# Seven products instead of eight for the second product of a token pair, with the third block's work moved between the pair's groups

## The chip, the cores and the metric

The kernel runs on one core of one Trainium2 chip. The metric is the device time of one execution in microseconds (us). All times here are of that one core. The engines are named as the profile names them: PE (TensorE, matrix products), PEld (its weight loads), DVE (VectorE), ACT (ScalarE), POOL (GpSimd) and SP (SyncE, which issues the transfers). L341 is line 341 of the kernel.

## The reference

Attention with a local window and block summaries feeds a first network of two gates, and that feeds a second network. The change concerns only the second network:

```python
def _moe2_ref(x, w_in, w_out):          # x: 1536 x 512, w_in: 512 x 2048, w_out: 2048 x 512
    h = x @ w_in
    relu6 = np.clip(h + 3.0, 0.0, 6.0)
    g = h * relu6 / 6.0
    return (g @ w_out).astype(np.float32)
```

The first network is `a = x @ w1; b = x @ w2; h = a * b @ w3; h @ w_out`, where `w3 @ w_out` is multiplied out beforehand in the kernel. The weights come as 64-bit numbers and are turned into 32-bit ones on the chip.

## The kernel before, in words

**Numbers.** Each 32-bit operand of a product is kept as a high and a low part (a slot of the arena holds both, 128 x 2 x 512), and `products` (L334 to L348) does three matmuls of 128x128 by 128x512 for each product of tiles: high by high, low by high, high by low. A high part is an ACT copy (L295, L555), the low part a subtraction on DVE or POOL (L298, L560). Twelve matmuls are the unit `GRP`.

**Stages.** The 1536 tokens are three blocks of 512. (1) Weights of the first network are multiplied out and the attention of the first block runs. (2) `ab` and `acc1` work through the first network, block after block, eight steps of 36 matmuls each, while the attention of the next block runs between; `x2_out` (L589) writes the block's result back as high and low parts. Meanwhile `convert_out` (L318) turns the 16 tiles of the second network's `w_out` into high and low parts and stores them in DRAM (`wo`). (3) The second network's first product for blocks 0 and 1 goes by Strassen's scheme, in eight groups q (L858 to L906): seven half products of 6 matmuls each in place of eight, on weight sums that `w_in_group` (L788) makes from two `w_in` tiles, and on token sums that `sums_of_x` (L772) makes once. `copied` (L825), `added` (L829) and `gated` (L835) put the seven results together, apply the gate and split it in high and low parts. Two of the four gated tiles of a group (block 0) go straight into `acc2` (L622), the second product, in the next group; the two of block 1 are stored in DRAM (`gj`), and so are the plain `w_in` tiles (`wi`). So a group is 42 matmuls of the first product and 24 of block 0's second product. (4) Block 2: 16 steps `hu` (L603, 12 matmuls) and 16 `acc2` (12 matmuls). (5) Block 1: 16 `acc2` on gated tiles read back from `gj`. The result of block 0 is written by `y_out` (L627) after the second `hu`, that of block 2 after its last `acc2`, that of block 1 at the end.

**Order of the work.** All instructions go into a list with an engine, an estimated duration and a due time; `Graph.schedule` (L92 to L150) simulates the engines and writes out one fixed order for each engine's queue. Only matmul groups bring their own due time; that of every other instruction follows from the matmuls that need it:

```python
        due = [o[2] if o[0] == "pe" else self.LAST for o in self.ops]
                due[i] = min(due[i], due[u] - self.ops[i][1] - self.LAT.get(e, 40))
```

Instructions marked `lock` (all of POOL, and DVE with its operands in SBUF) are simulated one at a time. On the chip each engine takes its queue in this order, and an instruction that waits holds all behind it.

Of the kernel before, what the change touches and what calls it, by code (L numbers as in the profile page):

```python
# [56 lines left out]
N_LATE, N_TMP = 4, 8  # L57
N_RAW, N_C = 4, 4


class Graph:
# [6 lines left out]
    LAT = {"sp": 2100, "pe": 250}  # L68
# [86 lines left out]
DUE_K, DUE_V, DUE_ROWS = 106.6, -119.0, -31.9  # L155
# [5 lines left out]
AHEAD, BEHIND = -27.8, -143.7  # L161
HOLD = 6000.0
OUT_AT, OUT_STEP = 180, 6.5


def build(tc, qd, kw, vw, kt, vt, consts, wp_in, w12_in, w2_in, out):
# [417 lines left out]
    def acc1(due, i, gs):  # L584
        for c in range(4):
            terms = [(wslice(A_WP + i, c * P), lambda h: slot(gs)[:, h, :])]
            products(due + c, terms, bank[c], c, both(A_WP + i) + both(gs), i == 0, i == NFC - 1)
# [14 lines left out]

    def hu(due, j, swin, gs):  # L603
        xs = A_X + NPAIR * j
        n = chain["n"]
        chain["n"] += 1
        b = 4 + n % 2
        terms = [(wslice(swin, k * P), lambda c, k=k: ar[:, xs + k, c, :]) for k in range(4)]
        products(due, terms, bank[b], b, both(swin) + [k for p in range(4) for k in both(xs + p)])
        t, u = ta[n % 2], tg[n % 2]  # L610
        g.op("act", 600, due, lambda: nc.scalar.activation(out=t, in_=bank[b], func=AF.Relu, bias=three),  # L611
             [("bank", b), "three"], [("ta", n % 2)])
        g.op(
            "dve", 685, due,
            lambda: nc.vector.scalar_tensor_tensor(  # L615
                out=u, in0=t, scalar=6.0, in1=bank[b], op0=ALU.min, op1=ALU.mult
            ), [("bank", b), ("ta", n % 2)], [("tg", n % 2)],
        )
        split(due, u, ("tg", n % 2), gs)
        return gs  # L620
# [60 lines left out]
    with tc.manual_schedule():  # L681
# [47 lines left out]
        for j in range(NBLK):  # L729
            for i in range(NFC):  # L730
                gs = ab(due, j, i)
                due += 2 * GRP
                if pend:
                    acc1(due, pend[1], pend[2])
                    if pend[1] == NFC - 1:
                        x2_out(due, pend[0])
                    due += GRP
                pend = (j, i, gs)
# [14 lines left out]
        def tile_of(n):  # L753
            return n // 2 + NFC * (n % 2)

        wo_slot = [A_LATE + i for i in range(N_LATE)] + [A_WP + i for i in range(NFC)]
        n_wo = len(wo_slot)
# [4 lines left out]
        half = GRP / 2  # L762

# [5 lines left out]
        def f32s(s, h):  # L769
            return lambda: slot(s)[:, h, :].bitcast(F32)  # L770

        def sums_of_x(due):  # L772

            for k in range(2):
# [7 lines left out]
                for n, o, a, b in ((1, 1, 0, 1), (3, 0, 2, 0), (2, 2, 2, 1), (4, 3, 3, 2)):  # L782
                    tensors(due, tf[o], tf[a], tf[b], ALU.subtract, fs[a], fs[b], fs[o])
                    s = tslot[n][k]
                    to_hi_lo(due, 1, tf[o], [fs[o]], lambda s=s: slot(s)[:, 0, :], lambda s=s: slot(s)[:, 1, :],
                             [("t", s, 0)], [("t", s, 1)], "dve")

        def w_in_group(due, q):  # L788

            w = [A_W2 + 4 * (q % 2) + i for i in range(4)]  # L790
            src = []
            for i in range(2):
                r, c, parts = to_f32(due, w2_in[q + NFC * i])
                src.append((lambda c=c: cs[c].bitcast(F32), ("c", c)))
            for i in range(2):
                src.append((lambda i=i: tmps[6 + i], ("f", 6 + i)))
            (a, ka), (b, kb), (e, ke), (f, kf) = src
            lo, hi = slice(0, TB // 2), slice(TB // 2, TB)
            for out, ko, x, kx, op, y, ky in (
                ((e, lo), ke, (b, lo), kb, ALU.add, (b, hi), kb),  # L800
                ((e, hi), ke, (e, lo), ke, ALU.subtract, (a, lo), ka),
# [108 lines left out]
        for n in range(n_wo - 8):  # L910
            at[n] = A_X + n
# [114 lines left out]
```

## Time and profile before

| | |
|---|---|
| Median of three runs | 572.25 us (569.72 to 572.67) |
| The profiled execution | 572.83 us, of which 570.9 us are the span from its first to its last instruction |
| PE busy | 537.8 us |
| DVE, ACT, POOL busy | 344.8, 281.9, 216.1 us |

Read the table of the engines first (who is busy), then the busy time by stage (where PE has gaps), then the chain of work that ended last (what the end hangs on), and only then the durations of single instructions. The columns of the views are named where they stand, in the section of rows.

### The profile page before, as it was taken

What the parts mean: (1) busy time and instruction counts of PE and PEld (TensorE: products, weight loads), DVE (VectorE), ACT (ScalarE), POOL (GpSimd) and SP (SyncE); (2) the same over time, 40 slices, a digit from 0 to 9 for tenths busy, and PEclk for the clock granted to TensorE, in tenths of its full rate; (3) what the DMA queues carried; (4) which work ended last, traced back from release to release, by engine and by line L of the source; (5) the groups of instructions that cost most, each with busy time, mean ns of one, the idle gap of its engine ahead of it and who ended that gap; (6) DMA issues with size and microseconds to landing.
All of it is one profiled execution on the core that took longest, in us unless ns stands there. A gap on an engine that the chain in (4) does not pass through costs nothing.

```text
span 570.9 us, 8140 instructions
## 1 busy us (share of the span) xinstructions
PE 537.8 (94%) x3032; PEld 437.3 (77%) x3032; DVE 344.8 (60%) x464; ACT 281.9 (49%) x483; POOL 216.1 (38%) x178
## 2 busy tenths in 40 slices
PE   0579999999989999999998999999999999999997
PEld 0457778887868887888886788888888888888885
DVE  5899977947673477879785888887645222220000
ACT  2688877535342445555646877775545222222001
POOL 0578646695431135377044866555100000000000
PEclk9999999999999999999999999999999999999999
DMA  8999883664232364568777857843499831002622
GB/s 308 379 356 324 240 269 105 189 204 153 70 92 86 111 214 145 182 228 258 249 258 261 291 205 288 299 169 148 148 337 419 312 110 38 1 0 85 203 82 73
DMA packets 42111, 112.62 MB, mean 197 GB/s; under 512 B 4040, under 2 KB 13512, under 8 KB 42072
## 3 DMA queue, kind: packets, MB, share of 16 engines
q1 hardware_dynamic: 41928, 111.97, 57.7%
q8 instruction: 24, 0.39, 0.3%
q10 hardware_dynamic: 144, 0.13, 0.1%
q14 instruction: 15, 0.12, 0.1%
HBM read 82.17 MB, written 28.31 MB: 194 GB/s over the span
## 4 chain that ended last, share of the span: by engine, by line
PE 83%; DMA 6%; DVE 4%; POOL 3%; ACT 2%; issue 2%; SPq 1%; ACTq 0%; DVEq 0%; POOLq 0%
PE bank L341 77%; PE bank L525 2%; DMA raw<-in_w_dram 2%; PE bank L463 2%; PE bank L510 1%; DMA kres<-in_kt_dram 1%; DMA qst<-in_q_dram 1%; POOL arena L298 1%; DMA wo<-raw 1%; DVE c L286 1%; POOL sc L500 1%; ACT c L267 0%; SPq L239 0%; DVE bank L282 0%; DVE sc L474 0%
## 5 line engine op out<-in xcount | busy, mean ns | idle before, releaser
L341 PE MATMUL bank<-arena 128*128 128x512 f32 x1152 | 278.2, 394 | 2.5 <-POOL arena L298 1.1
L341 PEld LDWEIGHTS bank<-arena 128*128 128x128 f32 x1152 | 214.6, 189 | 50.4 <-POOL arena L298 2.3
L341 PE MATMUL bank<-arena,w 128*128 128x512 f32 x816 | 196.6, 391 | 2.7 <-ACT ta L577 2.0
L341 PEld LDWEIGHTS bank<-arena,w 128*128 128x128 f32 x816 | 152.3, 188 | 36.2 <-ACT ta L577 2.9
L560 DVE TENSOR_TENSOR arena<-tg,arena 128x512 fp32r<-128x512 f32 x68 | 56.1, 825 | 26.3 <-ACT arena L555 25.5
L555 ACT ACTIVATE arena<-tg 128x512 fp32r<-128x512 f32 x72 | 45.1, 628 | 40.8 <-DVE tg L579 23.5
L282 DVE SCALAR_TENSOR_TENSOR c<-c,raw 128x512 uint32<-128x512 uint32 x48 | 45.0, 944 | 16.7 <-ACT raw L273 16.4
L298 POOL TENSOR_TENSOR arena<-c,arena 128x512 fp32r<-128x512 f32 (+1 forms) x34 | 42.0, 1249 | 33.5 <-ACT arena L295 33.5
L267 ACT ACTIVATE c<-raw 128x512 f32<-128x512 f32 x48 | 31.7, 665 | 33.2 <-DMA raw<-in_w_dram 27.2
L286 DVE SCALAR_TENSOR_TENSOR c<-raw,c 128x512 uint32<-128x512 uint32 x48 | 47.8, 1011 | 0.2
L273 ACT ACTIVATE raw<-raw 128x512 uint32<-128x512 uint32 (+1 forms) x72 | 46.8, 660 | 0.0
L341 PE MATMUL bank<-late,arena 128*128 128x512 f32 x192 | 46.6, 389 | 0.0
L298 POOL TENSOR_TENSOR raw<-c,raw 128x512 fp32r<-128x512 f32 x16 | 22.0, 1380 | 56.4 <-ACT raw L295 55.0
L341 PEld LDWEIGHTS bank<-late,arena 128*128 128x128 f32 x192 | 36.0, 188 | 7.5
L615 DVE SCALAR_TENSOR_TENSOR tg<-ta,bank 128x512 f32<-128x512 f32 x16 | 11.0, 689 | 50.3 <-ACT ta L611 50.3
L298 POOL TENSOR_TENSOR w<-c,w 128x512 fp32r<-128x512 f32 x24 | 35.7, 1491 | 11.7 <-ACT w L295 11.3
L611 ACT ACTIVATE ta<-bank,three 128x512 f32<-128x512 f32 x16 | 11.0, 687 | 48.8 <-PE bank L341 48.8
L579 DVE TENSOR_TENSOR tg<-ta,bank 128x512 f32<-128x512 f32 x24 | 16.3, 680 | 23.8 <-PE bank L341 23.8
L490 POOL TENSOR_TENSOR sc<-sc,st 128x960 f32<-128x960 f32 x12 | 22.3, 1856 | 22.1 <-DVE st L488 22.1
L577 ACT ACTIVATE ta<-bank 128x512 f32<-128x512 f32 x24 | 14.2, 591 | 33.2 <-PE bank L341 33.0
L639 DVE TENSOR_SCALAR c<-bank 128x256 f32<-128x256 f32 x1 | 0.4, 424 | 49.3 <-ACT c L637 49.3
L637 ACT ACTIVATE c<-bank 128x512 f32<-128x512 f32 (+1 forms) x12 | 6.8, 578 | 45.4 <-PE bank L341 45.2
(61 smaller groups left out, 514.0 us busy)
## 6 DMA issues: line engine op xcount, KB each, us to landing
raw<-in_w_dram SPq DMA_DIRECT2D x48, 512.0 KB, 4.7
raw<-in_wp_dram SPq DMA_DIRECT2D x22, 512.0 KB, 7.9
wo<-raw SPq DMA_DIRECT2D x16, 512.0 KB, 6.1
wi<-w SPq DMA_DIRECT2D x16, 512.0 KB, 5.2
gj<-arena SPq DMA_DIRECT2D x16, 512.0 KB, 5.1
w<-wi SPq DMA_DIRECT2D x16, 512.0 KB, 4.4
arena<-gj SPq DMA_DIRECT2D x16, 512.0 KB, 6.9
arena<-wo SPq DMA_DIRECT2D x12, 512.0 KB, 7.5
```

What stands on the lines that cost most here:

```text
L267: lambda uf=uf, wf=wf: nc.scalar.activation(out=uf, in_=wf[:, :, 1], func=AF.Copy, scale=2.0**-112),
L273: lambda lw=lw: nc.scalar.activation(out=lw, in_=lw, func=AF.Copy, scale=2.0**-29 * (1 - eps), bias=7.5 * eps - 0.5),
L282: lambda ui=ui, lw=lw: nc.vector.scalar_tensor_tensor(out=ui, in0=ui, scalar=3, in1=lw, op0=ALU.logical_shift_left, op1=ALU.bitwise_or),
L286: lambda ci=ci, ui=ui, hw=hw: nc.vector.scalar_tensor_tensor(out=ci, in0=hw, scalar=0x80000000, in1=ui, op0=ALU.bitwise_and, op1=ALU.bitwi ...
L298: lambda: e.tensor_tensor(out=lo(), in0=src(), in1=hi().bitcast(F32), op=ALU.subtract),
L341: nc.tensor.matmul(out=out_ap, lhsT=lhs(a), rhs=rhs(c), start=start and n == 0, stop=stop and n == 3 * len(terms) - 1, skip_group_check=skip,)
L463: nc.tensor.matmul(out=bank[bk[x]][o : o + D, p * NK : (p + 1) * NK], lhsT=qs[pr, x, p, :], rhs=ki[pr, p, lo : lo + NK], start=True, stop= ...
L490: lambda: nc.gpsimd.tensor_tensor(out=s8, in0=s8, in1=wide(0), op=ALU.subtract), [("st", i2)], skeys)
L555: g.op("act", 630, due, lambda: nc.scalar.activation(out=slot(s)[:, 0, :], in_=src_ap, func=AF.Copy), [src_key], [("t", s, 0)])
L560: lambda: eng.tensor_tensor(out=slot(s)[:, 1, :], in0=src_ap, in1=slot(s)[:, 0, :].bitcast(F32), op=ALU.subtract), [src_key, ("t", s, 0)], ...
L577: g.op("act", 600, due, lambda: nc.scalar.activation(out=a, in_=bank[4], func=AF.Copy), [("bank", 4)], [("ta", n % 2)])
L579: g.op("dve", 685, due, lambda: nc.vector.tensor_tensor(out=gf, in0=a, in1=bank[5], op=ALU.mult), [("bank", 5), ("ta", n % 2)], [("tg", n ...
```

## The change

The second product of blocks 0 and 1 also goes by seven products in place of eight, and it is computed transposed: the weights `w_out` are the stationary operand and the gated tiles (features x tokens) the moving one, so the two blocks' result leaves as `out^T` (512 x 1024) and is turned round on the host. It runs in one last stage, `LAST`: seven products one after another, each over eight steps k of 2 x 3 matmuls; a product's step takes one moving tile (a gated tile or the difference of two, split in high and low parts in that stage) and a half of a weight tile read from DRAM. Product 6 adds onto product 1's banks 4 and 5 after these were copied out, 7 and 4 likewise, and 3 onto product 5's banks 0 and 1.

The weight sums for it are made in the groups q by a new `w_out_group`: two `wo` tiles are read, added up on POOL, combined by four half-tile operations on POOL, split and stored as `ws`. The gated tiles of the pair stay 32-bit: one of four stays in a buffer (`held`), three are stored in DRAM as 128x512 (`gj`), without a split.

Block 2 no longer has a stage of its own: each group q has two steps `hu_last` (12 matmuls each, on the plain `w_in` tiles that the group holds anyway) and, in the next group, their two `acc2`. So `wi` is neither stored nor read. `w_in_group` makes its differences in place, after the plain tiles were split. The last block of the first network takes its steps in the order `LAST_ORDER`. The conversions `convert_out` begin at other times, and the groups 0 and 1 of `w_in` come after the eighth and the twelfth of them. Some of the planner's constants differ.

```diff
@@ -54,10 +54,13 @@
-N_LATE, N_TMP = 4, 8
+N_LATE, N_TMP = 0, 16
...
+LAT_SP = 2055.58
...
-DUE_K, DUE_V, DUE_ROWS = 106.6, -119.0, -31.9
+DUE_K, DUE_V, DUE_ROWS = 87.33, -119.0, -32.52
...
-AHEAD, BEHIND = -27.8, -143.7
-HOLD = 6000.0
-OUT_AT, OUT_STEP = 180, 6.5
+AHEAD, BEHIND = -17.94, -145.93
+HOLD = 5170.91
+SUMS_LATER = 10000.0
+OUT_LATER = 20000.0
+IN_AT = (8, 12)
+LAST_ORDER = (0, 1, 4, 5, 2, 3, 6, 7)
+OUT_AT, OUT_STEP = 180.54, 5.19
...
-    spilled = {
-        (n, i): dp.tile([P, 2, TB], F32, name=f"{n}{i}")
-        for n in ("wo", "wi", "gj") for i in range(NFC2)
-    }
+    spilled = {(n, i): dp.tile([P, 2, TB], F32, name=f"{n}{i}") for n in ("wo", "ws") for i in range(NFC2)}
+    spilled.update({
+        ("gj", j, h, i): dp.tile([P, TB], F32, name=f"gj{j}{h}{i}")
+        for j, h in ((0, 1), (1, 0), (1, 1)) for i in range(NFC)
...
+                i = LAST_ORDER[n_i] if j == NBLK - 1 else n_i
...
+        w_slots = [[A_W2 + 4 * p + i for i in range(4)] for p in range(2)]
+        o_slots = [[A_WP + 2 * p + i for i in range(2)] for p in range(2)]
+        s_slots = [A_X + NPAIR, A_X + NPAIR + 1]
         tslot = {n: [A_W1 + 2 * (n - 1) + k for k in range(2)] for n in range(1, 5)}
-        ring = [A_G, A_G + 1, A_G + 2, A_X + NPAIR, A_X + NPAIR + 1]
+        ring = [A_G, A_G + 1, A_G + 2]
...
+            w = w_slots[q % 2]
...
+            for i, (x, kx) in enumerate(src):
+                hi_lo_slot(due, x, kx, w[i], "pool")
+            (a, ka), (b, kb) = src
+            in_place(due, a, ka, b, kb, (
+                (("b", 1), ("b", 0), ALU.add, ("b", 1)),
+                (("b", 0), ("a", 0), ALU.subtract, ("b", 0)),
+                (("a", 0), ("b", 1), ALU.subtract, ("a", 0)),
+                (("a", 1), ("a", 1), ALU.subtract, ("a", 0)),
+            ), "pool")
+            for i, (x, kx) in enumerate(src):
+                hi_lo_slot(due, x, kx, w[2 + i], "dve" if i else "pool")
+        def w_out_group(due, q):
+            fs = []
             for i in range(2):
+                s = o_slots[q % 2][i]
+                fetch(due, s, ("wo", 2 * q + i))
+                k = ("f", 6 + i)
+                g.op("pool", 1290, due + SUMS_LATER,
+                     lambda i=i, s=s: nc.gpsimd.tensor_tensor(
+                         out=tmps[6 + i], in0=f32s(s, 0)(), in1=f32s(s, 1)(), op=ALU.add), both(s), [k])
+                fs.append((lambda i=i: tmps[6 + i], k))
+            (a, ka), (b, kb) = fs
+            in_place(due + SUMS_LATER, a, ka, b, kb, (
+                (("b", 1), ("a", 1), ALU.add, ("b", 1)),
+                (("a", 1), ("a", 0), ALU.subtract, ("a", 1)),
+                (("a", 0), ("b", 1), ALU.subtract, ("a", 0)),
+                (("b", 0), ("b", 0), ALU.subtract, ("a", 0)),
+            ), "pool")
+            for i, (x, kx) in enumerate(fs):
+                s = s_slots[i]
+                hi_lo_slot(due + SUMS_LATER, x, kx, s, "dve")
+                spill(due + SUMS_LATER, ("ws", 2 * q + i), lambda s=s: slot(s).bitcast(F32), both(s))
...
+        def hu_last(due, q, i, b):
+            n = chain["n"]
+            chain["n"] += 1
+            s, xs, gs = w_slots[q % 2][i], A_X + NPAIR * (NBLK - 1), ring[take("gs", len(ring))]
+            terms = [(wslice(s, k * P), lambda c, k=k: ar[:, xs + k, c, :]) for k in range(4)]
+            products(due, terms, bank[b], b, both(s) + [k for p in range(4) for k in both(xs + p)])
...
+            if n in IN_AT:
+                w_in_group(due, IN_AT.index(n))
+            convert_out(due + n // 2 * OUT_LATER, w2_in[NFC2 + tile_of(n)], ("wo", n),
+                        begin=(OUT_AT + OUT_STEP * n) * us)
         prev = []
+        bA, bB, bC, bD = 4, 5, 6, 7
         for q in range(NFC):
-            bA, bB, bC = (4 + (3 * q + i) % 4 for i in range(3))
+            bB, bC = bC, bB
...
+            def last_block(i):
+                nonlocal due
+                prev.append((2 * q + i, hu_last(due, q, i, bD)))
+                due += GRP
             step(1, bA, True)
             copied(due, bA, 0)
             step(5, bC, True)
-            filled()
+            if q:
+                last_block(0)
+            else:
+                filled()
             step(6, bA, False)
             copied(due, bA, 1)
-            filled()
             step(2, bB, True)
             h11 = added(due, bB, 0, 3)
-            prev.append((2 * q, gated(due, *h11)))
+            gated(due, *h11, *held(q))
+            filled(2)
             step(7, bA, False)
             copied(due, bA, 2)
             h22 = added(due, bC, 2, 4)
-            filled()
-            gated(due, *h22, spilled_as=2 * q + 1)
+            gated(due, *h22, *h22, spilled_as=("gj", 1, 1, q))
+            filled(2)
+            if not q:
+                last_block(0)
             step(4, bA, False)
-            prev.append((2 * q + 1, gated(due, lambda b=bA: bank[b], ("bank", bA))))
-            filled()
+            gated(due, lambda b=bA: bank[b], ("bank", bA), spilled_as=("gj", 0, 1, q))
+            last_block(1)
             step(3, bC, False)
             h12 = added(due, bC, 1, 5)
-            gated(due, *h12, spilled_as=2 * q)
+            gated(due, *h12, *h12, spilled_as=("gj", 1, 0, q))
+            if q == 0:
+                w_out_group(due, 0)
...
+        t_ring = [A_X + i for i in range(3 * NPAIR)] + [A_WP + i for i in range(4)]
+        h_ring = [(A_W2 + i // 2, i % 2) for i in range(16)]
+        LAST = (
+            (1, "wo", 0, 0, (4, 5), True), (2, "wo", 1, 0, (6, 7), True), (5, "ws", 1, 1, (0, 1), True),
+            (6, "ws", 0, 0, (4, 5), False), (7, "ws", 0, 1, (4, 5), False), (4, "wo", 1, 1, (4, 5), False),
+            (3, "ws", 1, 0, (0, 1), False),
+        )
+        y_t = out[0 : 2 * TB, :].rearrange("(d x) m -> d (x m)", x=2)
...
+        n_t = 0
+        for n, store, i, hh, bks, start in LAST:
+            last = n == LAST[-1][0]
+            done = []
+            for k in range(NFC):
+                b11, b21, b12, b22 = held(k), moved(0, 1, k), moved(1, 0, k), moved(1, 1, k)
+                other = (lambda k=k: tmps[6 + k % 2]), ("f", 6 + k % 2)
+                o, x, y = {
+                    1: (b11, None, None), 2: (b21, None, None), 3: (b22, None, None),
+                    5: (b11, b12, b11), 6: (b11, b22, b11), 7: (other, b22, b12), 4: (other, b21, b11),
+                }[n]
+                if x:
+                    tensors(due, o[0], x[0], y[0], ALU.subtract, x[1], y[1], o[1], "dve")
+                s = t_ring[n_t % len(t_ring)]
+                ws, wh = h_ring[n_t % len(h_ring)]
+                hi_lo_slot(due, o[0], o[1], s, "pool" if n_t % 2 else "dve")
+                n_t += 1
+                d = spilled[store, 2 * k + i]
+                g.op("sp", 700, due,
+                     lambda d=d, ws=ws, wh=wh, hh=hh: nc.sync.dma_start(
+                         out=slot(ws)[:, wh, :].bitcast(F32).rearrange("p (two n) -> p two n", two=2),
+                         in_=d[:, :, hh * H : (hh + 1) * H]),
+                     [(store, 2 * k + i)], [("t", ws, wh)])
+                done.append((s, ws, wh))
+                for m in range(2):
+                    if last and k >= NFC - 3:
+                        continue
+                    terms = [(lambda a, ws=ws, wh=wh, m=m: slot(ws)[:, wh, a * H + m * P : a * H + (m + 1) * P],
+                              lambda c, s=s: slot(s)[:, c, :])]
+                    products(due, terms, bank[bks[m]], bks[m], both(s) + [("t", ws, wh)],
+                             start and k == 0, k == NFC - 1, skip=not start)
+                    due += GRP / 4
...
+                if n == 1:
+                    copied(due, bks[m], m, 1.0 / 6.0)
+                elif n == 2:
+                    pair_out(due, 0, m, bks[m], m)
+                elif n == 6:
+                    copied(due, bks[m], 2 + m, 1.0 / 6.0)
+                elif n == 7:
+                    copied(due, bks[m], 4 + m, 1.0 / 6.0)
+                    pair_out(due, 1, 2 + m, m, 4 + m)
+                elif n == 4:
+                    pair_out(due, 0, 2 + m, bks[m])
+                elif n == 3:
+                    pair_out(due, 1, m, bks[m], 2 + m)
...
+    y = r.results[0]["out_0_dram"]
+    return np.concatenate([y[: 2 * TB].reshape(DM, 2 * TB).T, y[2 * TB :]])
```

## Rows read from the trace of the kernel before

**Rows 1.** The page: span; engines with busy time, share, instructions.
```profile
span 570.9 us, 8140 instructions
PE 537.8 (94%) x3032; PEld 437.3 (77%) x3032; DVE 344.8 (60%) x464; ACT 281.9 (49%) x483; POOL 216.1 (38%) x178
```
**Rows 2.** By stage: stretch, length, PE, PEld, DVE, ACT, POOL busy, clock, DMA share, GB/s.
```profile
170.00:310.00 140.00, 139.94 (x816) 114.12 (x816) 95.54 (x117) 67.10 (x115) 56.45 (x40) 1.00 0.60 198
310.00:325.00 15.00, 12.31 (x52) 9.24 (x52) 12.45 (x16) 12.20 (x23) 11.02 (x11) 1.00 0.82 275
325.00:567.00 242.00, 242.00 (x1068) 200.19 (x1067) 105.15 (x145) 99.65 (x167) 46.73 (x38) 1.00 0.47 174
```
**Rows 3.** End of the chain that ended last: start us, us, what.
```profile
324.81 242.41 PE bank L341 x1068
567.29 0.39 ACT c L637
567.71 0.42 DVE c L639
```
**Rows 4.** PE in order of time: start us, us, instructions [idle before <- releaser].
```profile
312.70 3.01 PE L341 MATMUL bank<-arena,w 128*128 128x512 f32 x12 [2.04 <-ACT ta L577]
...
321.72 6.58 PE L341 MATMUL bank<-arena,w 128*128 128x512 f32 x26 [0.57 <-ACT late_f L826]
```
**Rows 5.** The chain of waits ahead of those gaps.
```profile
297.36 7.03 DMA wo<-raw
304.40 4.30 DMA raw<-in_w_dram
```
**Rows 6.** PE's waits after 60 us: who, for whom, us in total, times, longest.
```profile
PE bank L525 <- ACT pt L517: 0.7, 1, 0.7
...
PE bank L341 <- ACT arena L538: 0.7, 1, 0.7
```
**Rows 7.** Groups by line and form: count | busy us, mean ns | idle before.
```profile
L560 DVE TENSOR_TENSOR arena<-tg,arena 128x512 fp32r<-128x512 f32 x68 | 56.1, 825 | 26.3 <-ACT arena L555 25.5
...
L555 ACT ACTIVATE arena<-tg 128x512 fp32r<-128x512 f32 x72 | 45.1, 628 | 40.8 <-DVE tg L579 23.5 <-DVE tg L615 11.6 <-DVE tg L844 5.4
...
L826 ACT ACTIVATE late_f<-bank 128x512 f32<-128x512 f32 x24 | 14.3, 595 | 14.9 <-PE bank L341 14.9
...
L780 POOL TENSOR_TENSOR late_f<-arena 128x512 f32<-128x512 f32 x8 | 12.9, 1633 | 2.0 <-DVE c L286 2.0
...
L615 DVE SCALAR_TENSOR_TENSOR tg<-ta,bank 128x512 f32<-128x512 f32 x16 | 11.0, 689 | 50.3 <-ACT ta L611 50.3
...
L767 DVE TENSOR_TENSOR late_f<-late_f,late_f 128x512 f32<-128x512 f32 x8 | 8.6, 1094 | 0.0
L767 POOL TENSOR_TENSOR late_f<-c,late_f 128x256 f32<-128x256 f32 x8 | 8.6, 1074 | 0.0
```
**Rows 8.** Single tile, duration ns min/median/max: differences on DVE, low parts on POOL.
```profile
L767 DVE TENSOR_TENSOR late_f<-late_f,late_f x8: 677/684/1797, 250.6 to 295.8; 128x512 f32<-128x512 f32 x8
...
L298 POOL TENSOR_TENSOR w<-late_f,w x8: 1295/1737/1748, 304.9 to 398.6; 128x512 fp32r<-128x512 f32 x8
```
**Rows 9.** As rows 2: one group q (66 matmuls, 15 us), then a stretch of block 2.
```profile
345.00:360.00 15.00, 15.00 (x68) 12.43 (x67) 12.86 (x17) 11.13 (x21) 8.70 (x7) 1.00 0.78 280
...
430.00:526.00 96.00, 96.00 (x425) 79.49 (x424) 25.28 (x37) 27.45 (x43) 0.00 (x0) 1.00 0.35 134
```
**Rows 10.** Transfers: count, KB each, median us from issue to landing.
```profile
raw<-in_w_dram SPq DMA_DIRECT2D x48, 512.0 KB, 4.7
...
out_dram<-c SPq DMA_DIRECT2D x11, 256.0 KB, 2.1
...
raw<-in_kt_dram SPq DMA_DIRECT2D x3, 512.0 KB, 4.2
...
out_dram<-c SPq DMA_DIRECT2D x1, 128.0 KB, 1.7
```
**Rows 11.** SP's issues at line 316, time on the queue, ns min/median/max.
```profile
L316 SPq DMA_DIRECT2D arena<-gj x16: 319/378/682, 418.3 to 545.5; - x16
```

More of the change, by code (lines that the diff above doesn't have):

```diff
@@ L582, in ab, with acc1 @@
         return gs
-    def acc1(due, i, gs):
+    def acc1(due, i, gs, n):
         for c in range(4):
             terms = [(wslice(A_WP + i, c * P), lambda h: slot(gs)[:, h, :])]
-            products(due + c, terms, bank[c], c, both(A_WP + i) + both(gs), i == 0, i == NFC - 1)
+            products(due + c, terms, bank[c], c, both(A_WP + i) + both(gs), n == 0, n == NFC - 1)
     def x2_out(due, j):
@@ L600, in x2_out @@
             )
[L603 to L620, printed above, removed]
     def acc2(due, n, gs, swout, cs_=range(4), b0=0):
@@ L729, in build @@
         for j in range(NBLK):
-            for i in range(NFC):
+            for n_i in range(NFC):
+                i = LAST_ORDER[n_i] if j == NBLK - 1 else n_i
                 gs = ab(due, j, i)
@@ L770, in f32s, with hi_lo_slot @@
             return lambda: slot(s)[:, h, :].bitcast(F32)
+        def hi_lo_slot(due, src, key, s, eng):
+            to_hi_lo(due, 1, src, [key], lambda: slot(s)[:, 0, :], lambda: slot(s)[:, 1, :],
+                     [("t", s, 0)], [("t", s, 1)], eng)
         def sums_of_x(due):
@@ L806, in w_in_group @@
-            for i, (x, kx) in enumerate(src):
-                s = w[i]
-                to_hi_lo(due, 1, x, [kx], lambda s=s: slot(s)[:, 0, :], lambda s=s: slot(s)[:, 1, :],
-                         [("t", s, 0)], [("t", s, 1)], "dve" if i == 3 else "pool")
-                if i < 2:
-                    spill(due, ("wi", 2 * q + i), lambda s=s: slot(s).bitcast(F32), both(s))
+            for i, (x, kx) in enumerate(src):
+                hi_lo_slot(due, x, kx, w[i], "pool")
+            (a, ka), (b, kb) = src
@@ new lines, in build @@
+        n_t = 0
+        for n, store, i, hh, bks, start in LAST:
+            last = n == LAST[-1][0]
+            done = []
+            for k in range(NFC):
+                b11, b21, b12, b22 = held(k), moved(0, 1, k), moved(1, 0, k), moved(1, 1, k)
[11 more added lines that the diff above has]
+                d = spilled[store, 2 * k + i]
+                g.op("sp", 700, due,
+                     lambda d=d, ws=ws, wh=wh, hh=hh: nc.sync.dma_start(
[11 more added lines that the diff above has]
+                    due += GRP / 4
+            for m in range(2):
+                if last:
+                    for s, ws, wh in done[NFC - 3 :]:
+                        terms = [(lambda a, ws=ws, wh=wh, m=m: slot(ws)[:, wh, a * H + m * P : a * H + (m + 1) * P],
+                                  lambda c, s=s: slot(s)[:, c, :])]
+                        products(due, terms, bank[bks[m]], bks[m], both(s) + [("t", ws, wh)],
+                                 False, s == done[-1][0], skip=True)
+                        due += GRP / 4
+                if n == 1:
[11 more added lines that the diff above has]
+                    pair_out(due, 1, m, bks[m], 2 + m)
```

148 lines of the change are left out of this document (67 added, 81 removed).

## The prediction

> **What bounds the kernel now.** The table of engines comes first: PE is busy for 537.8 of 570.9 us, and no other engine is busy for more than 60% [rows 1]. The stages show where the rest lies. From 325 us to the last matmul PE never stops: 1068 matmuls in 242 us, at the granted clock 1.00, the upper level of 2.4 GHz [rows 2]. From 170 to 310 us it is busy for 139.94 of 140 us; only around 310 to 325 us, where the second network begins, 2.69 us are missing [rows 2]. The chain that ended last says the same: one piece of 242.41 us of matmuls, then one ACT and one DVE piece and the last store [rows 3]. So from about 60 us on this is a stream of matmuls at 242.41 / 1068 = 0.227 us each [rows 3]. (The mean of one matmul in the profile is longer because neighbours overlap; I use the distance.) An edit here is worth the matmuls that it removes, less every wait that it puts into the stream.
>
> **What is removed.** Before, the pair's second product is 2 blocks x 16 tiles x 12 = 384 matmuls; after, 7 products x 8 steps x 6 = 336. All other products keep their counts, so 48 matmuls go, of one shape with those that stay: 48 x 0.227 = **10.9 us**, all of it in the stretch without gaps.
>
> **The groups q.** A group was 66 matmuls or 15.0 us and becomes 42 + 24 + 24 = 90 matmuls or 20.4 us. I take the busy times of a group before [rows 9] and add and take away instructions by their means [rows 7]. DVE: 12.86 - 4 splits x 0.825 + 2 gates x 0.689 + 4 low parts (two of block 2, two of the weight sums) x 0.825 = 14.2 of 20.4 us. ACT: 11.13 - 4 x 0.628 + 2 gates at about 0.69 (the DVE's duration taken for ACT, an estimate) + 4 x 0.628 = 12.5 of 20.4. POOL: 8.70 + 2 additions x 1.633 + 4 halves x 1.074 = 16.3 of 20.4. So DVE falls from 86% to 70%, ACT from 74% to 61%, and POOL rises from 58% to 80%: it becomes the fullest, but has room. The time that a bank has between its reading and its next use grows, too, since block 2's 12 matmuls stand between the halves. I cost the groups at nothing; the cover is 4 us of POOL in each group. If it is gone (four of the conversions are still to do in the first two groups, 4 x 1.74 us of POOL by the slower duration in [rows 8], or 3.5 us a group), PE would wait for a weight tile for at most some 1 to 2 us; that stands in the upper end.
>
> **The seam at 310 us.** The two gaps are 2.04 us behind ACT's copy at L577 and 0.57 us behind its copy at L826 [rows 4]. The first is one of queue order: ACT sat at a conversion whose load came after a store of 7.03 us and took 4.30 us itself [rows 5], and the copy stood behind it. The change puts the conversions of `w_in` groups 0 and 1 ahead of the last `wo` tiles, and frees two of the first network's weight slots two steps earlier, so this load has no such store right before it. But conversions 12 to 15 now fall into this stretch, and block 2's `x2_out` (four ACT copies of about 0.6 us and four DVE subtractions of about 0.69) must be done before the first `hu_last`, some 4.1 us (18 matmuls) later. I take back half of the 2.69 us, **-1.3**, between 0 and -2.7, and put **+0.3** (0 to 1.5) for `x2_out`.
>
> **Attention and start.** PE waits twice 0.7 us for the last attention tile of a block [rows 6]. `AHEAD` gives the attention after the first block due times 9.9 us earlier, so this can go: **-0.7**, between 0 and -1.4. `DUE_K`, `BEHIND`, `SUMS_LATER` and `OUT_LATER` are due times of instructions that are no matmuls, and the planner takes due times from matmuls alone, so they do nothing. The 44 ns of `LAT_SP`, `HOLD` and the new begin times can reorder the start: 0, between -1.5 and +1.5 (an estimate, the size of the gaps just named).
>
> **The last stage.** PE: 336 x 0.227 = 76.3 us. Beside it stand 56 splits and 32 differences. ACT: 56 x 0.628 = 35 us. DVE: 28 low parts x 0.825 + 32 differences x 1.094 = 58.1 us [rows 7]; POOL: 28 x 1.29 to 1.75 = 36 to 49 us [rows 8]. Each is under 76. They also run ahead: there are 16 moving slots, and the slots of the token sums and of block 2 come free from 18 us before the stage until its start, so products 1 and 2 (no differences) build up a lead of up to 16 steps or 21.8 us before the first difference is needed. SP: 24 reads of gated tiles, 56 of half weights and 8 stores at 0.378 us [rows 11] are 33 us; the queue is in order, but a half weight's slot comes free 16 steps before the stage needs it again. Transfers: 56 + 24 of 256 KB are 21 MB in 76 us, 276 GB/s; a group before moves 280 GB/s at a DMA share of 0.78 [rows 9], and loads of 1 KB runs (`raw<-in_kt`) land no later than those of 4 KB (4.2 against 4.7 us for 512 KB, [rows 10]). So the stage is costed at PE's time, plus two seams: product 7 adds onto banks 4 and 5 right behind 6, and 4 right behind 7, with the copies in between. The copy is 0.595 us [rows 7]; the matmuls of the other bank cover 0.68 us. Between the last matmul's end (324.81 + 242.41) and ACT's reading at 567.29 lie 0.07 us [rows 3], and twelve matmuls last up to 3.01 us where twelve distances are 2.72 [rows 4], so the last one ends up to 0.29 us after its successor could begin; 0.07 + 0.29 + 0.595 - 0.68 = 0.27 us is left if ACT is free, and 0.90 if it has just begun a split (+0.628). Two seams: 0.5 to 1.8, I take **+1.0**. No such pair stood bare before, hence both ends.
>
> **The tail.** Before: 0.39 + 0.42 us [rows 3] and a store of 128 KB (1.7 us, [rows 10]). After: one DVE operation of 0.689 and one store of 256 KB (2.1). -0.1 + 0.4 = **+0.3**.
>
> **Sum.** 572.83 - 10.9 - 1.3 + 0.3 - 0.7 + 1.0 + 0.3 = **561.5 us**. The profiled execution lies 0.58 us above the median of 572.25, less than the spread of the runs, so I leave it. Best bounds: -10.9 - 2.7 - 1.4 - 1.5 + 0.5 - 0.1, or 556.7; worst (without the two things taken back): -10.9 + 1.5 + 1.5 + 1.8 + 0.6 + 1.5 (a group), or 568.8.
>
> **Where the trace leaves doubt: DVE against POOL.** The same DVE difference took 0.684 us in the median and 1.797 at most, the same POOL low part 1.295 and 1.737 [rows 8]: each is stretched by about what the other lasts. The Trainium skill (SBUF — State Buffer, Who interferes with whom) says that DVE, with both inputs in SBUF, and GpSimd share a port pair under an exclusive lock, and the loser blocks fully. By that rule the two queues of the last stage add up: 60 x 0.684 + 28 x 1.295 = 77.3 us against PE's 76.3. That speaks against the change, since the stage that it makes denser was one in which POOL did nothing [rows 9].
>
> **Rivals.** (a) The sum of the two queues counts. Worked from rows alone, 60 undisturbed DVE operations and 28 POOL ones are 77.3 us. With the lead, that hides; without it (say the splits begin only with the stage, since the slots or the last weight sums come late), the last split is done at 77 us and its product 1.4 us later, and the first product starts some 2 us late: 3 to 7 us of waits, **564.5 to 568.8 us**. For it: POOL at 80% in the groups before. Against it: a group before held 12.86 us of DVE and 8.70 of POOL in 15 us with PE at 15.00 [rows 9].
> (b) The gain is used up: waits of 8 to 13 us in groups and last stage together, **570 to 575 us**, no change. It needs the same in both places, POOL late in the groups by 0.7 us in each of eight and the last stage without a lead.
> (c) Slower: in the last stage every DVE operation loses its turn to a POOL one. At 1.797 us [rows 8] the 60 operations are 108 us, 31 more than PE's 76.3, less a lead of 5 us that the slots leave: 561.5 + 26 = **about 588 us**. It beats the forecast's gain where the mean DVE operation there passes (76.3 + 5 + 14) / 60 = 1.6 us; the means in the trace are 0.825 and 1.094 [rows 7].
> (d) The change doesn't do what it says, and the matmuls don't get fewer. Against it, the counts in the code; it would give 572 us and falls under (b).
>
> **How the numbers follow.** Forecast with its bounds (556.5 to 564.5) 0.65; (a) 0.19; (b) with (d) 0.07; (c), with its smaller sizes above 575 us, 0.06; below 556.5 us 0.03. The range 556.5 to 568.8 holds 0.84 of that; without (a) it would hold too little. Half a percent, 2.9 us, is about what a measurement of this kernel can tell from no change. Faster by more (below 569.4): 0.65 + 0.19 + 0.03 = 0.87; within: 0.07; slower: 0.06.
>
> **What would show it.** 48 fewer products in the count of PE (3032 to 2984). PE full from the seam to the end, at 1.00 and 0.227 us a matmul. The seam at the start of the second network with one gap at most. In the last 76 us two gaps of PE under 1 us each, behind an ACT copy of a bank. DVE and POOL differences in the last stage with means under 1.2 and 1.75 us. The prediction is wrong if PE in the last stage or in the groups waits for a split (L298, an ACT high part) or for a half weight from DRAM over and over, or if the stretch up to 310 us moves by more than 3 us.

## The result, and the profile of the changed kernel

The changed kernel takes 563.97 us (median of four runs, 563.5 to 565.47) against 571.15 us before (four runs, the fourth at 570.05): the ratio is 0.988, with a 95% interval of 0.984 to 0.992. The forecast was 561.5 us in a range of 556.5 to 568.8, so it was faster as forecast and inside the range, 2.5 us above the forecast. As a gain it fell further short. The forecast's sum takes 11.3 us off the profiled execution of the kernel before, 572.83 us, which is longer than all four timed runs. The medians differ by 7.2 us, and the spans of the two profiled executions by 9.3. The profiled execution of the changed kernel took 563.58 us.

The page of the changed kernel (as [rows 1]) has 48 instructions less on PE, and the stages (as [rows 2]) show where PE has gaps now; the last line is a stretch of the kernel before.

```profile
span 561.6 us, 8360 instructions
PE 529.9 (94%) x2984; PEld 431.0 (77%) x2984; DVE 408.2 (73%) x513; ACT 304.8 (54%) x523; POOL 308.7 (55%) x254
```

```profile
120.00:142.00 22.00, 18.50 (x102) 14.28 (x101) 12.17 (x15) 9.16 (x16) 17.50 (x24) 0.92 0.52 172
142.00:313.00 171.00, 171.00 (x1100) 139.74 (x1099) 119.57 (x151) 79.88 (x136) 79.56 (x57) 1.00 0.42 141
313.00:481.00 168.00, 166.85 (x735) 137.51 (x734) 125.75 (x153) 103.24 (x177) 107.84 (x94) 1.00 0.66 223
481.00:558.00 77.00, 76.89 (x337) 62.55 (x335) 51.68 (x56) 30.93 (x52) 31.72 (x21) 1.00 0.61 191
```

```profile
120.00:142.00 22.00, 22.00 (x157) 17.78 (x156) 15.78 (x21) 10.60 (x18) 14.98 (x22) 1.00 0.57 173
```

The gaps of [rows 4] around 310 us and of [rows 6] near 167 us are gone (142 to 313 us is full), and the last 77 us are full. In their place stand a hole of 3.5 us between 120 and 142 us, with a lower clock, and 1.15 us of waits in the groups. PE's waits of the changed kernel after 60 us (who, for whom, us in total, times, longest):

```profile
PE bank L471 <- ACT vall L429: 1.9, 1, 1.9
PE bank L349 <- DVE tg L587: 1.6, 1, 1.6
PE bank L349 <- ACT late_f L844: 1.1, 2, 0.7
PE bank L349 <- DVE arena L665: 0.7, 1, 0.7
PE bank L349 <- POOL arena L306: 0.3, 1, 0.3
```

**The hole at 126 us**, in order of time, all engines (start, us, instruction [idle before <- releaser]):

```profile
120.30 0.55 SPq L247 DMA_DIRECT2D raw<-in_kt_dram  x1
...
126.27 1.22 DVE L366 TENSOR_REDUCE ksum<-raw 128x32 f32<-128x1024 f32 x1 [2.23 <-DMA raw<-in_kt_dram]
127.41 0.68 DVE L587 TENSOR_TENSOR tg<-ta,bank 128x512 f32<-128x512 f32 x1
...
128.14 3.01 PE L349 MATMUL bank<-arena,w 128*128 128x512 f32 x12 [1.58 <-DVE tg L587]
...
137.28 1.16 PE L471 MATMUL bank<-kall,qst 64*64 64x120 f32 x28 [1.92 <-ACT vall L429]
```

The third load of the second batch's keys is issued at 120.30 and lands 6 us later. DVE's maximum over those keys (L366) waits for it 2.23 us, the gate of the first network (L587) stands behind it in DVE's queue, and PE needs the gate's bank. SP is held, too, so four loads of weights go out only at 127.5 us, ACT stands at their conversion, and PE waits 1.92 us more. Behind that the granted clock falls (the column before the last two; 0.5 is the lower level of 1.2 GHz):

```profile
136.00:138.00 2.00, 0.72 (x26) 0.75 (x28) 1.27 (x2) 2.00 (x5) 1.59 (x2) 1.00 0.00 0
138.00:140.00 2.00, 2.00 (x15) 1.43 (x7) 1.65 (x4) 1.93 (x4) 0.00 (x0) 0.52 0.18 38
140.00:142.00 2.00, 2.00 (x8) 1.54 (x7) 1.43 (x2) 0.00 (x0) 1.93 (x2) 0.63 0.92 282
```

**The sum, from the two traces.** The second network begins at 312.70 us before and at 313.24 after: +0.5. From there to the end of the last matmul it is 254.52 us before and 244.67 after: -9.85. From there to the end of the span it is 3.7 us both times. -9.85 + 0.5 is the difference of the spans, 570.9 - 561.6.

### The profile page after: what moved, and what is told of

Its sections match the earlier page's. It is cut to its first block, busy times and chain, and to the rows that moved or that the text cites. A ratio compares the mean times of both kernels' runs of the same rounds, so it can differ in the third digit from the quotient of the medians.

```text
span 561.6 us, 8360 instructions
## 1 busy us (share of the span) xinstructions
PE 529.9 (94%) x2984; PEld 431.0 (77%) x2984; DVE 408.2 (73%) x513; ACT 304.8 (54%) x523; POOL 308.7 (55%) x254
## 4 chain that ended last, share of the span: by engine, by line
PE 69%; DMA 17%; DVE 5%; ACT 4%; issue 2%; POOL 2%; SPq 1%; ACTq 0%; DVEq 0%; POOLq 0%
PE bank L349 65%; DMA raw<-in_w_dram 3%; DMA raw<-in_wp_dram 3%; DMA gj<-tg 2%; PE bank L533 2%; DMA ws<-arena 2%; PE bank L471 2%; DMA wo<-raw 2%; DVE c L294 1%; DMA kres<-in_kt_dram 1%; DMA qst<-in_q_dram 1%; PE bank L518 1%; DMA kall<-in_kw_dram 1%; DMA raw<-in_kt_dram 1%; DMA arena<-gj 1%
## 5 line engine op out<-in xcount | busy, mean ns | idle before, releaser
L349 PE MATMUL bank<-arena,w 128*128 128x512 f32 x1152 | 269.2, 391 | 2.7 <-DVE tg L587 1.6
L349 PEld LDWEIGHTS bank<-arena,w 128*128 128x128 f32 x1152 | 216.0, 188 | 50.0 <-ACT late_f L844 3.0
L349 PE MATMUL bank<-arena 128*128 128x512 f32 x960 | 234.4, 397 | 1.1 <-DVE arena L665 0.7
L349 PEld LDWEIGHTS bank<-arena 128*128 128x128 f32 x960 | 179.7, 190 | 41.0 <-issue 1.5
L303 ACT ACTIVATE arena<-late_f 128x512 fp32r<-128x512 f32 x64 | 39.3, 627 | 33.5 <-DVE late_f L759 18.1
L306 DVE TENSOR_TENSOR arena<-late_f,arena 128x512 fp32r<-128x512 f32 x44 | 38.8, 884 | 13.8 <-ACT arena L303 13.3
L306 POOL TENSOR_TENSOR arena<-late_f,arena 128x512 fp32r<-128x512 f32 x20 | 29.4, 1473 | 31.1 <-PE bank L349 12.6
L815 POOL TENSOR_TENSOR late_f<-arena 128x512 f32<-128x512 f32 x16 | 23.1, 1447 | 29.2 <-DVE arena L306 21.8
L587 DVE TENSOR_TENSOR tg<-ta,bank 128x512 f32<-128x512 f32 x24 | 16.3, 681 | 24.3 <-PE bank L349 24.3
L303 ACT ACTIVATE w<-c 128x512 fp32r<-128x512 f32 x40 | 24.7, 624 | 15.0 <-POOL c L759 5.7
L759 DVE TENSOR_TENSOR late_f<-arena,late_f 128x512 f32<-128x512 f32 x24 | 27.4, 1168 | 5.2 <-DMA arena<-gj 5.0
```

The costliest lines, as they stand in the source:

```text
L303: lambda: nc.scalar.activation(out=hi(), in_=src(), func=AF.Copy), keys, khi)
L306: lambda: e.tensor_tensor(out=lo(), in0=src(), in1=hi().bitcast(F32), op=ALU.subtract),
L349: nc.tensor.matmul(out=out_ap, lhsT=lhs(a), rhs=rhs(c), start=start and n == 0, stop=stop and n == 3 * len(terms) - 1, skip_group_check=skip,)
L759: lambda: e.tensor_tensor(out=out(), in0=a(), in1=b(), op=op), [ka, kb], [ko], True)
L815: lambda i=i, s=s: nc.gpsimd.tensor_tensor(out=tmps[6 + i], in0=f32s(s, 0)(), in1=f32s(s, 1)(), op=ALU.add), both(s), [k])
```

## The experiments

Each kernel ran beside the kernel before on the same chip; in those runs the kernel before took 570.0 to 570.3 us. The brackets give the ratio to it and its 95% interval. The changed kernel's own 563.97 us were taken beside a kernel before of 571.15 us, so a difference to it is given by the medians and by the ratios, and the two need not agree.

**e1 and e2: one constant.** e1 is the changed kernel with the due times of the later attention tiles put back, e2 the kernel before with the new ones alone.

```diff
-AHEAD, BEHIND = -17.94, -145.93
+AHEAD, BEHIND = -27.8, -145.93
```

> The changed kernel with one constant put back, the due times of the later attention tiles (AHEAD -27.8 in place of -17.94). Theory: the earlier due times moved four loads of an attention tile ahead of the third load of keys on SP's queue, DVE's maximum over those keys stood 2.2 us ahead of a gate, and PE lost two gaps of 3.5 us around 126 to 138 us and some 1.1 us to a half clock behind them. Putting the constant back takes these 4.6 us away and may bring back the 1.4 us of waits for the last attention tile: a median of 559.5 to 561 us against 564.0, PE full from 120 to 140 us. Rival: the order there comes from the other constants (latency of SP, begin times): stays at 564 with the gap.

> The kernel before with that one constant alone (AHEAD -17.94). Theory: it gets the same gap near 126 to 138 us without any of the rest of the change, and loses the waits of 1.4 us near 167 us: 573 to 576 us, slower than before by 2 to 5 us. Rival (the forecast's view, the earlier due times help): 569.5 to 570.5 us.

e1 took 559.86 us (0.982, 0.981 to 0.984), e2 577.26 us (1.012, 1.010 to 1.014). So the constant costs the changed kernel 4.1 us by the medians, 3.2 by the ratios (0.988 to 0.982) and 3.6 by the spans of the two traces. On the kernel before, where the whole planner's order can shift with it, it costs 7.0 us by the medians, more than the 2 to 5 expected. PE in e2, in order of time, has the same two gaps, and e1's stretch is full:

```profile
127.04 3.02 PE L341 MATMUL bank<-arena,w 128*128 128x512 f32 x12 [1.03 <-DVE tg L579]
...
137.31 1.29 PE L463 MATMUL bank<-kall,qst 64*64 64x120 f32 x28 [2.90 <-ACT vall L421]
```

```profile
120.00:142.00 22.00, 22.00 (x158) 17.70 (x157) 16.29 (x20) 10.52 (x18) 15.01 (x22) 1.00 0.55 169
```

SP's queue shows why. In e1 the third load of keys goes out at 116.14 us, ahead of the loads of the next attention tile (`kall`, `qst`, `vall`); with the new constant these four go first. e1 has the 1.4 us of [rows 6] near 167 us again, so the constant does take them away, at two to three times their price. It also waits 0.7 us at 243 us and 1.4 us near 466 us.

**e3 and e4: a second pair of slots for the weight sums.** In the groups of the changed kernel PE waits twice for the copy at L844. In front of the first wait ACT stood 6 us at the high part of a weight sum, since the only pair of slots for these sums was still being stored:

```profile
380.95 0.63 ACT L303 ACTIVATE arena<-late_f 128x512 fp32r<-128x512 f32 x1 [5.99 <-DMA ws<-arena]
...
382.58 0.58 ACT L844 ACTIVATE late_f<-bank 128x512 f32<-128x512 f32 x1
```

```profile
383.22 1.66 PE L349 MATMUL bank<-arena,w 128*128 128x512 f32 x6 [0.46 <-ACT late_f L844]
```

```profile
469.91 5.30 PE L349 MATMUL bank<-arena,w 128*128 128x512 f32 x22 [0.69 <-ACT late_f L844]
```

```diff
-        s_slots = [A_X + NPAIR, A_X + NPAIR + 1]
+        s_slots = [[A_X + NPAIR, A_X + NPAIR + 1], [A_WP + 6, A_WP + 7]]
...
-                s = s_slots[i]
+                s = s_slots[q % 2][i]
```

> The changed kernel with two pairs of slots for the sums of the second product's weights, by turns, in place of one. Theory: the two waits of PE in the groups (0.46 and 0.69 us, behind the copy at L844) come from ACT standing at a high part of such a sum until the last store of that slot has landed; with a second pair both vanish and the time falls by 1 to 1.5 us to 562.5 to 563. Rival: ACT then stands at another wait (a load of raw weights) and the time stays at 564.

> The changed kernel with both edits, the old AHEAD and two pairs of slots for the sums. Theory: the two savings lie in different stretches and add up: 558.5 to 560 us. Rival: the planner's order shifts and new waits take one of them back: 560.5 to 562 us.

Neither saved anything: e3 took 566.17 us (0.992, 0.990 to 0.994), 2.2 us more than the changed kernel, and e4 565.84 us (0.992, 0.991 to 0.994), 6.0 us more than e1. In e3 the two waits did go, but waits of 2.2 us at 479 us and of 1.0 in the last stage came in their place. In e4 PE has no wait from 243 to 475 us, but it waits in the last stage. PE there, and then ACT, in order of time:

```profile
525.23 20.07 PE L349 MATMUL bank<-arena,w 128*128 128x512 f32 x76 [5.28 <-ACT late_f L844]
```

```profile
523.48 1.21 ACT L303 ACTIVATE arena<-late_f 128x512 fp32r<-128x512 f32 x2 [2.00 <-DVE late_f L759]
524.60 0.58 ACT L844 ACTIVATE late_f<-bank 128x512 f32<-128x512 f32 x1
```

The copy of product 6's bank stands in ACT's queue behind high parts of product 7's tiles, and these wait for differences on DVE (L759), of which two take 2.31 us there:

```profile
521.66 2.31 DVE L759 TENSOR_TENSOR late_f<-arena 128x512 f32<-128x512 f32 x2
```

This is the first of the two seams that the prediction priced at 0.5 to 1.8 us together; here it alone is 5.3.

**e5: the order of the seam alone.** The kernel before, with `LAST_ORDER` and the two `w_in` groups after the eighth and twelfth conversion.

```diff
+                i = LAST_ORDER[n_i] if j == NBLK - 1 else n_i
...
+            if n in IN_AT:
+                w_in_group(due, IN_AT.index(n))
```

> The kernel before with the order of the seam alone: the last block's steps by LAST_ORDER, and the groups 0 and 1 of w_in after the eighth and the twelfth conversion. Theory: ACT no longer stands behind a load of w_in that follows a store, the gap of 2.04 us at 310 us closes and perhaps the one of 0.57 too: 567.5 to 568.5 us against 570.3. Rival: the gap closed in the changed kernel because its later work is due later, not by this order: it stays at 570 to 571 us.

It took 579.73 us (1.016, 1.013 to 1.018), a miss on both sides. The gap at 310 us did close: PE runs from 294 to 340 us without a wait. But PE waits at other places now. PE in order of time:

```profile
241.63 1.98 PE L527 MATMUL bank<-pt,vall 120*64 120x64 f32 x32 [2.77 <-ACT pt L519]
...
342.87 2.55 PE L343 MATMUL bank<-arena,w 128*128 128x512 f32 x6 [3.00 <-ACT late_f L829]
...
350.79 2.11 PE L343 MATMUL bank<-late,arena 128*128 128x512 f32 x8 [1.11 <-DVE arena L562]
```

The chain of waits ahead of 350 us is a store `wo<-raw` of 5.11 us and a load of 3.97 us before ACT's conversion, as in [rows 5], only 40 us later, in the groups of 15 us. Ahead of 241 us it is a load of raw weights, 4.59 us. Behind these waits the granted clock is down, too: 0.89 from 230 to 260 us and 0.84 from 340 to 351. So the order closes the seam and moves its cause; that the changed kernel's groups of 20.4 us take it in is argued from its full stretch there, not shown by a run of its own.

**e6 and e12: less room to run ahead in the last stage.** 4 and 2 moving slots (places for the split tiles that the products read) in place of 16; e6 with the new `AHEAD`, e12 with the old one. With 2 slots the last three steps of product 3, which are kept together, read tiles that have been written over, so e12's result is not what is asked there.

```diff
-        t_ring = [A_X + i for i in range(3 * NPAIR)] + [A_WP + i for i in range(4)]
+        t_ring = [A_X + i for i in range(4)]
```

> The changed kernel with 4 slots for the moving tiles of the last stage in place of 16, so that no lead can build up. Theory (DVE and POOL lose time to each other and only the lead hides it): two steps need about 2 x 1.2 us of differences and 0.9 us of low part on DVE, or 3.3 us, against PE's 2.72; over the four products with differences (16 pairs of steps) PE waits some 6 to 12 us, 570 to 576 us. Rival (each engine by itself is under PE, no lead is needed): 564 to 566 us.

> The changed kernel with the old AHEAD and only 2 moving slots. A slot is then free for the next split only when the product of two steps before is done, so difference, high part, low part and their hand-overs (0.69 + 0.63 + 0.7 to 1.8 us and some 0.3 us) must fit in one step of 1.36 us beside the other slot's. Theory: they do not; a pair of steps takes 3.3 to 4.3 us in place of 2.72 and the stage grows by 15 to 40 us: 573 to 598 us. Rival (the engines' own order hides it even so): 557 to 562 us.

e6 took 561.53 us (0.985, 0.984 to 0.987): faster than the changed kernel by 2.4 us by the medians and 1.4 by the ratios, not slower by 6 to 12. My theory that only the lead hides DVE and POOL fell. The traces differ in three places. The two waits of the groups are gone (PE is full from 140 to 520 us), 1.6 us. The last 384 matmuls take 0.9 us more, 88.9 against 88.0. And 1.8 us are gained ahead of the second network, where the edit has no instruction: the hole of 3.6 us is there, but the clock stays at 1.00 behind it, and from its end to the second network e6 needs 174.4 us against 176.0. So of the gain only the groups' part can be put down to the slots. The stretch with the hole in e6:

```profile
120.00:140.00 20.00, 16.40 (x100) 12.76 (x99) 13.89 (x15) 8.81 (x15) 14.92 (x23) 1.00 0.49 158
```

The differences of the last stage are not stretched in e6. By line and form, the changed kernel's last stage first, then e6's (count | busy, mean ns):

```profile
L306 POOL TENSOR_TENSOR arena<-late_f,arena 128x512 fp32r<-128x512 f32 x16 | 24.1, 1507 | 22.7 <-ACT arena L303 11.3 <-PE bank L349 8.0 <-DMA w<-wo 3.3
L759 DVE TENSOR_TENSOR late_f<-arena,late_f 128x512 f32<-128x512 f32 x19 | 23.2, 1254 | 4.5 <-DMA arena<-gj 4.4
...
L759 DVE TENSOR_TENSOR late_f<-arena 128x512 f32<-128x512 f32 x7 | 7.1, 1041 | 0.1
```

```profile
L759 DVE TENSOR_TENSOR late_f<-arena,late_f 128x512 f32<-128x512 f32 x18 | 11.9, 681 | 0.0
```

e12 took 574.23 us (1.007, 1.005 to 1.009), 14.4 us over e1, as its theory said, near its lower edge of 573: with two slots a tile's steps do follow one another on the path. So the last stage needs a lead of a few steps, and has nearly all of it with four slots.

**e7: no POOL in the last stage.** e4 with all its low parts on DVE.

```diff
-                hi_lo_slot(due, o[0], o[1], s, "pool" if n_t % 2 else "dve")
+                hi_lo_slot(due, o[0], o[1], s, "dve")
```

> The kernel of e4 (old AHEAD, two pairs of sum slots), with all low parts of the last stage on DVE and none on POOL. In e4 PE waited 5.3 us in the last stage for a bank's copy that stood behind high parts of tiles whose differences were late. Theory (the differences are late because they lose turns to POOL): alone, DVE needs 32 x 0.69 + 56 x 0.69 = 61 us of 76, the wait goes and the time is 559 to 561 us. Rival (they are late because the stored tiles land late at the stage's start): the wait stays, 564 to 567 us.

It took 565.13 us (0.992, 0.990 to 0.994), as e4. The differences fell to 0.688 us, the wait at product 7 from 5.28 only to 2.72, and the waits near 475 us, where product 5's first tiles come, grew from 0.64 to 2.05 us:

```profile
L759 DVE TENSOR_TENSOR late_f<-arena,late_f 128x512 f32<-128x512 f32 x20 | 13.8, 688 | 4.5 <-DMA arena<-gj 4.2
```

```profile
526.38 34.91 PE L349 MATMUL bank<-arena,w 128*128 128x512 f32 x144 [2.72 <-ACT late_f L844]
```

So what POOL takes from DVE is about half of that wait, and not the rest. For the rest the rival, a late start of the stage, fits, as e7's chain ahead of 475 us begins with a store `ws<-arena` of 6.71 us and a read of a gated tile of 3.00; that is argued from the chain, not shown by a run. The time did not fall, since the waits near 475 us grew and the granted clock behind them was 0.72 from 475 to 481 us, where e4 kept 1.00.

**e8, e9 and e11: the wait at the start of the last stage.** e1 has one more wait of 1.4 us near 466 us. e8 tells the planner that product 5's differences are ready 4 us later, e9 is e1 with 4 moving slots, e11 is e4 with 4.

```diff
-                    tensors(due, o[0], x[0], y[0], ALU.subtract, x[1], y[1], o[1], "dve")
+                    g.op("dve", 690, due, lambda o=o, x=x, y=y: nc.vector.tensor_tensor(
+                        out=o[0](), in0=x[0](), in1=y[0](), op=ALU.subtract), [x[1], y[1]], [o[1]], True,
+                        slack=4000 if n == 5 else 0)
```

> The kernel of e1 (the changed one with the old AHEAD), with the planner told that product 5's differences are ready 4 us later than it reckons. In e1 PE waited 1.4 us near 466 us for a copy of a bank; ACT stood at a gate, this behind a DVE addition, and that behind the first of these differences, whose stored tile landed 5 us after its issue. Theory: the difference moves behind the additions of the last group, the wait goes and the time falls from 559.9 by 1 to 1.5 us to 558.3 to 559. Rival: the next DVE or ACT instruction waits for the same crowd of transfers there, 559.5 to 560.5 us.

> The changed kernel with the old AHEAD (as e1) and 4 moving slots in the last stage (as e6). Theory, formed after e6: the work that runs ahead of the last stage does harm, since it puts ACT and DVE behind transfers that land late while the last groups still need them; so PE has no gap from 300 us to the end, and the two savings (4.1 and 2.4 us) add up: 557 to 558.5 us. Rival: the wait near 466 us in e1 comes from other work and stays: 559.5 to 560.5 us.

> The kernel of e4 (old AHEAD, two pairs of sum slots) with 4 moving slots. Theory (what runs ahead does the harm): the second pair of sum slots hurt e4 only because it let more work run ahead; with 4 slots the wait of 5.3 us goes and the time is that of e9, 557 to 558.5 us. Rival (the second pair itself does harm, by its place or by the stored tiles that must wait for it): 561 us or more.

e8 took 561.57 us (558.31 to 563.83; 0.985, 0.982 to 0.987), e9 562.02 (0.986, 0.984 to 0.988), e11 562.93 (0.987, 0.985 to 0.989). All three are misses against 559.86. PE at that place in e1 and in e9, and the wait of e8:

```profile
466.29 5.76 PE L349 MATMUL bank<-arena,w 128*128 128x512 f32 x24 [1.40 <-ACT late_f L844]
```

```profile
466.68 7.36 PE L349 MATMUL bank<-arena,w 128*128 128x512 f32 x24 [1.80 <-ACT late_f L844]
```

```profile
PE bank L349 <- DVE arena L568: 2.6, 1, 2.6
```

The wait changes its place with each edit and stays, and what it hangs on changes, too. In e1 DVE stands 4.17 us for a gated tile; in e9 ACT stands 2.50 us for the store of a sum. In e8 the chain is the store of a sum and, at its end, two subtractions on DVE that take 1.63 and 1.69 us, each beside a low part on POOL (0.68 us without one):

```profile
464.30 7.41 DMA ws<-arena
...
474.26 1.63 DVE arena L306
475.89 1.69 DVE arena L568
```

The theory formed after e6 does not hold: with four slots PE waits 1.80 us in e9 where e1 waits 1.40. Of the 3.0 us between the spans of the two (561.0 and 558.0), 1.6 are the clock, on the 24 matmuls behind the wait. e8's runs go with the clock as well: 558.31 us at a mean granted clock of 1.000, 563.83 at 0.991, and 0.9% of 560 us are 5.0 of those 5.5 (an estimate). So its median says little, but the wait in its trace did not go.

e11 is 2.9 us better than e4, so part of what the second pair of slots did there was to let more run ahead. All of these kernels have the same crowd of transfers there: stores of sums, reads of gated tiles and weight halves. From 455 to 475 us the DMA share is 1.03 at 378 GB/s in the changed kernel, 1.01 in e1, but also 1.02 in e6, which has no wait. What decides between them is left open.

**e10: what a product is worth.** e9 without product 4 of the last stage.

```diff
-            for k in range(NFC):
+            for k in range(0 if n == 4 else NFC):
```

> The kernel of e9 with product 4 of the last stage left out, its 48 matmuls, 8 differences, 8 splits and 8 loads (so the lower half of block 0's transposed result is not what is asked). Theory: with PE as the bound each matmul is worth its distance, 48 x 0.227 = 10.9 us, and one seam of at most 0.3 us: 10.7 to 11.3 us under e9. Rival (DVE or the transfers bound the stage): less than 9 or more than 12.5 us.

It took 550.02 us (0.966, 0.963 to 0.969), 12.0 us under e9, between the two expectations. In the traces the last stage is 77.8 us for 336 matmuls in e9 and 66.1 for 288 in e10 (their waits taken off), 11.7 us; and e9's 24 matmuls after its wait took 7.36 us, partly at the lower clock, 1.6 more than e1's 24, which e10 was spared. So the 48 matmuls are worth their distance and 0.8 us. I put these down to short waits of a stage with four slots, as e6's last 384 matmuls take 0.9 us more than the changed kernel's; no run shows it by itself. The stage is bound by PE.

## Why the prediction was right, point by point

- **The 48 matmuls (10.9 us): right.** From the second network's start to the last matmul, with the waits taken off (0.73 us before; 0.62 and 0.86 us after, by the distance of the matmuls), it is 253.8 us against 243.2: 10.6 us. The missing 0.3 us are of the size of the last stage's seams. e10 shows the price of a product by itself.
- **The groups (0, at worst 1.5): the worst came, by another way.** POOL was not the cause: it is busy for 64% from 313 to 481 us, not 80%. The waits (1.15 us, 1.5 by the distance of the matmuls) hang on the copy at L844 behind high parts that wait for a store or a gated tile.
- **The seam at 310 us (-1.3 and +0.3): better than forecast.** Both gaps went, 2.6 us (2.8 by the distance). The cause was read rightly; e5 shows that the order by itself only moves it.
- **Attention (-0.7, bounds 0 to -1.4): the step that failed.** The 1.4 us of [rows 6] did go, but the same constant opened a hole of 3.5 us at 126 us and a stretch at the lower clock, some 1.1 us (what is left of the sum: 313.24 - 312.70 = 3.5 + 1.1 - 2.0 - 1.4 - 0.6 us of other waits). e6, whose clock stayed at 1.00 behind the same hole, shows 1.5 us for that stretch. I took an earlier due time for a gain without asking what is moved behind it on SP's queue, and put the bound at zero. e1 shows its price, 3.2 to 4.1 us. Without it the kernel takes 559.86 us, 1.6 below the forecast, and gains 10.4 us where the sum says 11.3.
- **The last stage (0, seams +1.0): right, and less.** The 48 matmuls of product 7, up to the seam with product 4, took 11.16 us, 0.26 over their distance: the 0.27 that the prediction gave for a seam with ACT free. The chain's last pieces (start, us, what):

```profile
524.63 11.16 PE bank L349 x48
535.80 22.11 PE bank L349 x96
557.94 0.69 DVE c L997
```

- **The tail (+0.3): 0.** 3.7 us before and after.
- **DVE against POOL, and rival (a).** The rule of the Trainium skill (SBUF — State Buffer, Who interferes with whom) is borne out in the durations: the differences take 1.25 us in the mean beside POOL, 0.68 in e6. The Trainium skill says "fully blocks" there of DVE's two-port modes, and of an instruction with two inputs in SBUF that it contends; e8 shows the full wait for such a one. The last stage of the changed kernel hides it, as the forecast had it: PE is busy for 76.89 of 77 us there. But it is not harmless in general, and rival (a) was no idle one: in e4 about half of the 5.3 us at product 7 went with POOL's share (e7), and e4's 565.84 us lie in that rival's range; in e8 it stretched the two subtractions that PE waited for. Rival (c), at about 588 us, needed a mean of 1.6 us; the splits and differences on DVE have 1.04.
- **The sum: in part luck.** In the traces the change gains 9.3 us, not 11.3. Attention and the groups came out 5.4 us worse than the forecast's terms; the seam at 310 us, the seams of the last stage, the tail and waits that the sum did not have came out 3.4 us better. That the time lay inside the range owes something to this, as 3.2 us of attention alone were outside its bounds of -1.4 to 0.

## What to carry to other kernels

In a kernel that is one stream of matmuls, count the matmuls first: the gain is their number by their distance. Then go through every constant of the order as a change of its own, ask what it puts in front of what on the transfer queue, and who stands behind that; here one of them took back about a third of what the algorithm gave (3.2 to 4.1 of 10.9 us). Room to run ahead is neither good nor bad in itself: with 4 slots in place of 16 two waits of the groups went in e6, and in e9 the same edit took none away; with 2 slots the stage was 14.4 us longer. Last, look at the granted clock before you put a difference of 2 us down to an edit.

## What the runs showed of the hardware

The clock did not fall behind each gap of PE. After the 1.8 us of e9, 24 matmuls took 7.36 us, with a granted clock of 0.50 from 468 to 470 us; after the 1.4 us of e1, 5.76; e8, with 2.6 us some 11 us later, kept 1.00. Behind the gaps of 1.6 and 1.9 us near 126 and 137 us the changed kernel's clock was 0.52 and then 0.63; e6, with gaps of 1.1 and 2.5 us at the same places, kept 1.00. What decides it is not shown.

In e8 a subtraction on DVE with both inputs in SBUF waited until the POOL instruction beside it was done: POOL's low parts end at 475.34 and 477.02 us, and the two subtractions that lie across them end 0.55 us later each, at 475.89 and 477.57, where one alone takes 0.68.

A load of 512 KB landed in 4.2 us in the kernel before (the median of three, [rows 10]) and in 6.0 at 126 us here, behind two others.
